# k's fourth block by seven products, with pieces of the second x^T phi(k) batch between them

## The chip, the cores and the metric

One core of a Trainium2 chip. The metric is the device time of the whole kernel in microseconds (us), lower is better. Matrix products run on TensorE (PE), element-wise work on VectorE (DVE) and ScalarE (ACT); SyncE (SP) and GpSimd (POOL) issue the transfers that are spoken of here.

## The reference

Cut to what matters here: x (2048 x 640) goes through a linear attention with 32 heads and through a gated unit, and a sigmoid gate mixes the two.

```
qkv = x @ wqkv;  q, k, v = split(qkv)
phi = lambda t: where(t > 0, t + 1, exp(t)) + 1e-6
kv = einsum("hsd,hse->hde", phi(k), v)
z = einsum("hsd->hd", phi(k))
a = einsum("hqd,hde->hqe", phi(q), kv) / (einsum("hqd,hd->hq", phi(q), z) + 1e-6)
b = (sigmoid(x @ w_gate) * (x @ w_up)) @ w_down
g = sigmoid(x @ gate_w)
out = g * (a @ wo) + (1 - g) * b
```

The part that is changed computes k = x @ wk for some tokens, and x^T phi(k), from which kv follows later.

## The kernel before

Every fp32 product is made of three matmuls of rounded fp32 halves: a tensor is split into a high half (ACT, a copy that rounds) and a low half (DVE, the difference). `mm3` issues the three, `split` the two halves; their lines are the helpers' L202 and L204 (matmul), L214 (ACT) and L218 (DVE, two tensors).

The first phase (to about 134 us) computes k and x^T phi(k). The columns of x^T (640 features, KC = 5 groups of 128) come in chunks of CW = 256 tokens: `xst[:, 0]` has the chunk of one 512-token group, `xst[:, 1]` the matching chunk of the next group. A block is 128 tokens of either side; so a chunk has two blocks, and there are eight blocks (0 to 7) in four chunks. k of a block has two sides (`xst[:, 0]` and `xst[:, 1]`) and two column halves of HW = 322 (320 of k and two columns for the gate), which makes a 2 x 2 block product over the features, plus a fifth feature group:

- `KPlain(b)` computes it plainly: 5 groups x 2 sides x 2 halves x 3 matmuls = 60 matmuls of 322 columns, into four PSUM banks (ch, dd, cc, rot).
- `KBlock(b)` computes it by seven products in Winograd's manner, `s1` to `s7`: 18 terms x 3 = 54 matmuls, into three banks (ch, dd, cc). ch and cc are added to from product to product and copied out between them (`s1`, `s3` and `s5` end with an ACT copy of ch). It needs sums of x's four blocks (tiles xt0 to xt3: `Chunk.sum`, `Chunk.form`) and sums of k's weights (`k_sum`, `k_form` into ksh and ksl), and the difference of the fifth weight rows (`k_fifth_d`, into k5h[2] and k5l[2], read by `s7`).

Before, blocks 0 to 3 are plain and 4 to 7 by seven products, two blocks at a time (a's product, then b's). The plain blocks keep x's groups 0 and 1 of the second side in xt0 (`plain_b12`).

`phi` of a side turns a block's banks into phi(k) (two exp, two relu on ACT, one combining operation on DVE: kr for the first side, kb for the second), `k_split` splits it (pkh, pkl), and `GTBatch.part(u, t0, t1)` adds tokens' products x^T phi(k) into bank u: seven parts (GU), six matmuls of 512 columns (parts 0 to 4) or 320 columns (5 and 6) for each block. The tokens' x (xnst) is split too (xnh, xnl; `queue_xn`). The sum over phi(k) goes by POOL transfers into zacc. A part that is complete is added into gta or gtb by DVE.

There are two PSUM banks of each name (ch, dd, cc, rot), taken in turn: the third tile of a name waits until the readers of the first are done.

The order on each engine is fixed when the program is built. The PE order is the code's order. Splits and sums are queued (`order.add`, `queue_...`) and put between the matmuls by `order.fill()` according to estimated costs, or at once by `order.need(key)`, which issues everything queued up to that key. At run time each engine works through its own list in order and waits for its inputs by semaphores; SP's transfers wait in their list the same way. The next chunk of x is loaded by `chunks[2].load`, behind the loads of xnst in SP's list; each of these is issued when the split that reads its buffer before it is done.

Of the kernel before, what the change touches and what calls it, by code (L numbers as in the profile page):

```python
# [15 lines left out]
P = 128  # L16
S, D, F = 2048, 640, 1536
H, DH = 32, 20
KC = D // P
# [4 lines left out]
HW = HALF + 2  # L24
# [144 lines left out]
def a_cost(w):  # L169
    return 0.19 + w * 0.00084  # L170


def v_cost(w):
    return 0.155 + w * 0.00104
# [3 lines left out]
def gated_mix_kernel(ctx: ExitStack, tc: tile.TileContext, xt, xn, wk, wv, wo, wst_q, wst_f, out_t):  # L178
# [6 lines left out]
    order = Order()  # L185

    def f32(ap):
        return ap.bitcast(F32)
# [23 lines left out]
    def act(out, src, fn, after="", **kw):  # L212
        order.on_act(width(out), after)
        nc.scalar.activation(out, src, fn, **kw)  # L214
# [5 lines left out]
    def vec3(out, a, scalar, b, op0, op1, after=""):  # L220
        order.on_vec(width(out), after)
        nc.vector.scalar_tensor_tensor(out, a, scalar, b, op0=op0, op1=op1)
# [64 lines left out]
    def op_tile(tag, dt=F32R):  # L287
        return p1.tile([P, 2 * HW], dt, name=tag, tag=tag, bufs=6)
# [120 lines left out]
    xc = XForms(px)  # L409
    xc.turned(px)  # L410
    XF = {1: xc}
    b12h, b12l = xc.ft[0]
# [8 lines left out]

    xst_v = [xst[:, b] for b in range(2)]
    chunks = [Chunk(pr, c, xc, xst_v) for pr in range(2) for c in range(TG // CW)]
    for ck in chunks[:2]:
        ck.b12 = (b12h, b12l)
    wk_st = [op_tile(t, F32) for t in ("xnh", "xnh", "xnl", "pkh", "pkl")]
    for k in range(KC):
        nc.sync.dma_start(xst[:, 0, k], xt[0, :, k, :CW])
# [11 lines left out]
    def k_sum(s, j):  # L440
        a11, a21 = wk_st[j][:, lo_h], wk_st[j][:, hi_h]
        a12, a22 = wk_st[2 + j][:, lo_h], wk_st[2 + j][:, hi_h]
        if s == 0:
            add(a22, a21, a22)
        elif s == 2:
            sub(a21, a11, a21)
        elif s == 1:
            sub(a11, a22, a11)
        else:
            sub(a12, a12, a11)  # L450

    def k_form(s, j):
        src = (wk_st[2 + j][:, hi_h], wk_st[j][:, lo_h], wk_st[j][:, hi_h], wk_st[2 + j][:, lo_h])[s]
        split(ksh[:, s, j], ksl[:, s, j], src)
# [19 lines left out]
            return k1h[:, k], k1l[:, k]  # L474
        return (k3h[:, k], k3l[:, k]) if k < 2 else (k2h[:, k - 2], k2l[:, k - 2])

    def queue_ks():
        for s, sums in ((1, (0, 2, 1)), (0, ()), (2, ()), (3, (3,))):
            for j in range(2):
                for t in sums:  # L480
                    order.add(0, v_cost(HW), lambda t=t, j=j: k_sum(t, j))
            for j in range(2):
                order.add(a_cost(HW), v_cost(HW), lambda s=s, j=j: k_form(s, j), ("ks", s))
        order.add(a_cost(HW), 2 * v_cost(HW), k_fifth_d, ("ks", 5))

    XN, PK, KR = {}, {}, {}
    xn_st = {}
# [1 line left out]
    def tok(b, side):  # L489

        pr, j = divmod(b, 4)
        return (2 * pr + side) * 4 + j
# [8 lines left out]
    def split_xn(n):  # L501
        xh, xl = op_tile("xnh"), op_tile("xnl")
        split(xh[:, :D], xl[:, :D], xn_st.pop(n)[0])
        XN[tok(n // 2, n % 2)] = (xh, xl)
        order.then(lambda: load_xn(n + 2))

    def queue_xn(b):
        for n in (2 * b, 2 * b + 1):
            order.add(a_cost(D), v_cost(D), lambda n=n: split_xn(n), ("xn", b), lambda n=n: xn_st[n][1])
# [116 lines left out]
    def k_split(i, after=""):  # L626
        r = KR.pop(i)
        ph, pl = op_tile("pkh"), op_tile("pkl")
        vh, vl = (t[:, :D].rearrange(view2, j=2) for t in (ph, pl))
        act(vh, r, AF.Copy, after, bias=EPS)  # L630
        at = order.act

        def low():
            order.vec = max(order.vec, at)
            vec3(vl, r, EPS, f32(vh), OP.add, OP.subtract)
        order.then(low)
        PK[i] = (ph, pl)
# [10 lines left out]
    def z_step():  # L648

        n = z_tree.pop(0)  # L650
        if n < 0:
            for d in range(4):
                nc.gpsimd.dma_start(z4[d * H:(d + 1) * H], z_dram[:4].rearrange("r (h u d) -> d h u r", u=KC, d=4)[d])
        elif n == 0:
            nc.gpsimd.dma_start(z_dram, zacc[:32])
        else:
            t = zacc if n > 16 else z_dram
            nc.gpsimd.dma_start(t[:n], t[n:2 * n], accum_op=OP.add)

    def queue_split(b):  # L660
        for s in range(2):
            order.add(a_cost(D), v_cost(D), lambda s=s: k_split(tok(b, s)), ("pk", b))
# [46 lines left out]
    def load_w():  # L709
        if w_loads and w_loads[0] in w_hold:  # L710
            w_skipped.append(1)
        elif w_loads:
            n = kind, i = w_loads.pop(0)
            t = pg.tile([P, 2, D], F32, name="wst", tag="wst", bufs=2)
            if kind == "f":
                nc.sync.dma_start(t, wst_f[i, :, 0:2])
            elif kind == "q":
                nc.sync.dma_start(t, wst_q[:, 2 * (i % 2):2 * (i % 2) + 2])
            else:
                nc.sync.dma_start(t[:, 0], wst_q[:, KC - 1])  # L720
            WST[n], W_AT[n] = t, max(order.pe, order.vec) + 4.0
# [62 lines left out]
    def queue_su(n):  # L784
        def fn():
            w_form(n, "V", WST[n][:, 1, :4 * P])
            order.then(load_w)
        order.add(a_cost(4 * P), v_cost(4 * P), fn, ("V", n), lambda: w_free("V"))
# [46 lines left out]
    b1.phi_a()  # L835
    b1.phi_b()
    chunks[1].queue(sums=False)
    queue_xn(1)
    queue_split(1)
    g = GTBatch(0, [0])  # L840
# [6 lines left out]
    batches = {1: [1, 2], 2: [3, 4], 3: [5, 6]}  # L847

    for c in range(1, 4):
        ck = chunks[c]  # L850
        if c == 1:
            a, b = KPlain(2), KPlain(3)
            order.need((ck, "plain"))
            queue_ks()
            queue_xn(2)
            for k in range(KC):
                a.k(k)
                order.fill()
            a.phi_a()
            for k in range(KC):  # L860
                b.k(k)
                order.fill()
                if k == 0:
                    a.phi_b()
            order.need(("ks", 5))
            for t in range(2):
                k_split(tok(2, t))
        else:
            a, b = KBlock(2 * c), KBlock(2 * c + 1)
            for n in range(1, 6):  # L870
                order.need((ck, n))
                if c == 2 and n >= 3:
                    order.need(("ks", (1, 0, 2)[n - 3]))
                getattr(a, f"s{n}")()
                getattr(b, f"s{n}")()
                if n == 2:
                    queue_xn(2 * c)
            order.need((ck, 6))
            if c == 2:
                order.need(("ks", 5))  # L880
            if c + 1 < len(chunks):
                chunks[c + 1].load()
            else:
                nx = [Chunk(0, i, None, xst_v) for i in range(2)]
            a.s6()
            a.s7()
            a.sum_b()
            a.phi_a()
            b.s6()
            a.phi_b()  # L890
            order.need(("pk", 2 * c - 1))
            k_split(tok(2 * c, 0))
            b.s7()
            b.sum_b()
            k_split(tok(2 * c, 1))
        if c == 3:
            pa_cm.__exit__(None, None, None)
            pg_cm = tc.tile_pool(name="pg", bufs=1, side="right", reuse_waits="tile")
            pg = pg_cm.__enter__()
            for _ in range(2):  # L900
                load_w()
        elif c == 1:
            chunks[2].load(lag=6.0)
        g = GTBatch(c, batches[c])
        order.need(("xn", 2 * c))
        if c < 3:
            chunks[c + 1].queue()
        else:
            queue_xn(7)
        held = 3 if c < 3 else 4  # L910
        for u in range(held):
            g.part(u, 0, 2, ("rot", "dd", "ch", "cc")[u])
            if u == 0:
                b.phi_a()
            if u == 1:
                b.phi_b()
        queue_split(2 * c + 1)
        if c < 3:
            queue_xn(2 * c + 1)
        else:  # L920
            queue_w(("u", 1))
            queue_w(("q", 0))
            queue_su(("q", 0))
        for u in range(held):
            g.part(u, 2, 3)
            order.fill()
        for u in range(GU):
            g.part(u, 3 if u < held else 0, 4)
            order.fill()
            if c == 3 and u == 5:  # L930
                z_step()
# [327 lines left out]
    last = QLast(1)  # L1259
# [12 lines left out]
    for n, b in enumerate(blocks):  # L1272
# [20 lines left out]
        else:  # L1293
            last = QLast(0)
# [587 lines left out]
    for turn in SEQ:  # L1882
# [5 lines left out]
        for i, q, pp in jobs:  # L1888
            b = now[i]
            k = hk + pp * len(now) + i  # L1890
# [55 lines left out]
```

## Time and profile before

| | us |
|---|---|
| time, median of 3 runs (lowest to highest) | 728.12 (727.79 to 728.7) |
| the profiled execution's own time | 727.9 |
| its span | 726.2 |
| PE busy | 721.5 |
| DVE busy | 486.4 |
| ACT busy | 320.4 |
| POOL busy | 129.1 |

The time is that of the whole launch; the span runs from the first to the last instruction in the trace, and all starts below are counted from its beginning. Block 2 stands at 31.69 to 40.59 on PE, block 3 at 40.59 to 49.49, the batch of blocks 1 and 2 at 49.49 to 66.88, and blocks 4 and 5 at 66.88 to 82.90. A row in order of time gives the start, the duration, the engine, the line, the operation, out<-in, the shape, and in brackets the idle time before it and what ended it.

### The profile page before, as it was taken

The page shows a single profiled execution, that of the slowest core. Times are in us where ns is not written, and L with a number is a line of the kernel's source. Part 1 is how long each engine was busy: PE and PEld are TensorE (multiplying, and loading weights), DVE is VectorE, ACT ScalarE, POOL GpSimd, SP SyncE. Part 2 cuts the span into 40 slices and gives each one's busy share as a digit, 9 for nine tenths or more (in the row PEclk, how much of TensorE's full clock was granted, in tenths as well). Part 3 has the DMA queues.
Part 4 walks back from the last instruction along what each step waited for, and adds up shares of the span by engine and source line. Part 5 has one row for each costly group of instructions (what it writes and reads, how often), then busy time and mean ns, then how long its engine had stood idle before and what let it go on. Part 6 is the DMA issues. An engine that isn't in the chain of part 4 may idle for free.

```text
span 726.2 us, 9528 instructions
## 1 busy us (share of the span) xinstructions
PE 721.5 (99%) x3411; PEld 608.9 (84%) x3411; DVE 486.4 (67%) x773; ACT 320.4 (44%) x541; POOL 129.1 (18%) x221
## 2 busy tenths in 40 slices
PE   9999999999999999999999999999999999999997
PEld 8999998888888888888888888888888888888886
DVE  4878576868773788678879778796866664434340
ACT  5764628167766233332323242233366644424321
POOL 0311010222430023113224223340200000010000
PEclk9999999999999999999999999999999999999999
DMA  7553537697545464656578658474988966466431
GB/s 253 126 145 76 163 55 212 144 309 228 204 159 196 152 215 137 185 190 226 197 255 314 223 187 288 160 269 130 323 305 264 330 224 194 156 210 198 147 113 72
DMA packets 62563, 144.05 MB, mean 198 GB/s; under 512 B 11150, under 2 KB 24494, under 8 KB 62517
## 3 DMA queue, kind: packets, MB, share of 16 engines
q1 hardware_dynamic: 43829, 88.50, 38.7%
q0 software_dynamic: 18544, 54.83, 23.2%
q8 instruction: 26, 0.43, 0.3%
q14 instruction: 20, 0.16, 0.1%
q10 hardware_dynamic: 144, 0.13, 0.1%
HBM read 89.81 MB, written 49.84 MB: 192 GB/s over the span
## 4 chain that ended last, share of the span: by engine, by line
PE 99%; DVE 0%; ACT 0%; issue 0%
PE ch L204 18%; PE cc L204 17%; PE rot L204 16%; PE dd L204 14%; PE ch L202 9%; PE cc L202 8%; PE rot L202 8%; PE dd L202 7%; PE cc L1131 1%; PE rot L295 1%; PE cc L1212 0%; DVE ot L218 0%; ACT ot L214 0%
## 5 line engine op out<-in xcount | busy, mean ns | idle before, releaser
L218 DVE TENSOR_TENSOR hf<-hw,hf 128x1024 fp32r<-128x1024 f32 x54 | 65.8, 1223 | 68.8 <-ACT hf L214 68.6
L214 ACT ACTIVATE hf<-hw 128x1024 fp32r<-128x1024 f32 x54 | 56.8, 1057 | 54.5 <-PE rot L204 32.1
L218 DVE TENSOR_TENSOR c<-cc,c 128x512 f32<-128x512 f32 x56 | 37.7, 686 | 46.2 <-PE cc L204 40.5
L204 PE MATMUL ch<-hf,wa 128*128 128x512 f32 x160 | 49.3, 389 | 0.0
L204 PE MATMUL dd<-hf,wa 128*128 128x512 f32 x160 | 49.3, 389 | 0.0
L1732 POOL DMA_DIRECT2D out_t<-ot x18 | 9.7, 540 | 183.8 <-DVE ot L218 180.8
L214 ACT ACTIVATE wG<-wst 128x640 fp32r<-128x640 f32 x17 | 12.4, 737 | 65.0 <-PE dd L204 65.0
L214 ACT ACTIVATE c<-ch 128x512 f32<-128x512 f32 x32 | 19.1, 597 | 49.6 <-PE ch L204 44.8
L204 PE MATMUL rot<-hf,wa 128*128 128x512 f32 x128 | 39.4, 389 | 0.0
L204 PE MATMUL cc<-hf,wa 128*128 128x512 f32 x128 | 39.4, 389 | 0.0
L202 PE MATMUL dd<-xrh,wG 128*128 128x512 f32 x90 | 35.4, 394 | 0.0
L204 PEld LDWEIGHTS ch<-hf,wa 128*128 128x128 f32 x160 | 30.0, 188 | 6.3
L204 PEld LDWEIGHTS dd<-hf,wa 128*128 128x128 f32 x160 | 30.0, 188 | 6.3
L204 PE MATMUL dd<-xrh,wG 128*128 128x512 f32 x90 | 35.0, 389 | 0.0
L204 PE MATMUL dd<-xrl,wG 128*128 128x512 f32 x90 | 35.0, 389 | 0.0
L218 DVE TENSOR_TENSOR c<-c,om 128x512 f32<-128x512 f32 x48 | 33.1, 692 | 1.6
L202 PE MATMUL cc<-xbh,wS 128*128 128x512 f32 x84 | 32.7, 389 | 0.0
L204 PE MATMUL cc<-xbl,wS 128*128 128x512 f32 x84 | 32.7, 389 | 0.0
L204 PE MATMUL cc<-xbh,wS 128*128 128x512 f32 x84 | 32.7, 389 | 0.0
L202 PE MATMUL dd<-hf,wa 128*128 128x512 f32 x80 | 31.1, 389 | 0.0
L202 PE MATMUL ch<-hf,wa 128*128 128x512 f32 x80 | 31.1, 389 | 0.0
L214 ACT ACTIVATE c<-rot 128x512 f32<-128x512 f32 x24 | 14.2, 597 | 38.3 <-PE rot L204 31.0
(471 smaller groups left out, 2088.5 us busy)
## 6 DMA issues: line engine op xcount, KB each, us to landing
hf<-p_dram SPq DMA_DIRECT2D x16, 512.0 KB, 5.3
hw<-h1T SPq DMA_DIRECT2D x16, 512.0 KB, 5.0
hw<-h0T SPq DMA_DIRECT2D x16, 512.0 KB, 4.5
wst<-wst_f SPq DMA_DIRECT2D x12, 640.0 KB, 4.5
xst<-xt SPq DMA_DIRECT2D x10, 640.0 KB, 7.5
h1T<-c POOLq DMA_DIRECT2D x24, 256.0 KB, 2.7
h0T<-c POOLq DMA_DIRECT2D x24, 256.0 KB, 3.1
hw<-h1B SPq DMA_DIRECT2D x11, 512.0 KB, 4.6
```

Of the source, the lines that this page charges most:

```text
L202: nc.tensor.matmul(o, l_hi, r, start=first, stop=False, skip_group_check=True)
L204: nc.tensor.matmul(out, a, b, start=False, stop=last and n == 1, skip_group_check=True)
L214: nc.scalar.activation(out, src, fn, **kw)
L218: nc.vector.tensor_tensor(out, a, b, op=op)
L295: nc.tensor.matmul(wps[:, :w], ones_w[:, :P], ones_w[:, :w], start=True, stop=True)
L1131: nc.tensor.matmul(ps[:w, b0:b1], v[:, m, :w], g(m), start=(m == 0), stop=(m == KC - 1))
L1732: (eng or nc.gpsimd).dma_start(out_t[o * P:(o + 1) * P, g * TG + c0:g * TG + c1], t[:, c0:c1])
```

## The change

Block 3 becomes a `KBlock` while block 2 stays plain. The second half of chunk 1 (128 tokens of either side) gets a chunk object of its own, `half[1]`, whose sums and splits are queued behind the plain splits; `half[0]` has block 2's plain split of x's groups 0 and 1. The sums and splits of k's weights, queued after block 1 as before, are queued in two pieces around `half[1]`'s. Parts 0, 1 and 2 of the batch of blocks 1 and 2 are started for block 1 between the products of block 3: part 0 and part 1 after `s2`, part 2 after `s4`. phi and the split of block 2 stand between the products as well, phi of block 3's first side after `s6`, that of its second side after `s7`.

```diff
-    for ck in chunks[:2]:
-        ck.b12 = (b12h, b12l)
+    chunks[0].b12 = (b12h, b12l)
+    half = [Chunk(0, 2 + i, xc, [x[:, :, i * P:(i + 1) * P] for x in xst_v], P, (b12h, b12l)) for i in range(2)]
...
-    def queue_ks():
-        for s, sums in ((1, (0, 2, 1)), (0, ()), (2, ()), (3, (3,))):
+    def queue_ks(end):
+        for s, sums in ((3, (3,)),) if end else ((1, (0, 2, 1)), (0, ()), (2, ())):
...
-        order.add(a_cost(HW), 2 * v_cost(HW), k_fifth_d, ("ks", 5))
+        if end:
+            order.add(a_cost(HW), 2 * v_cost(HW), k_fifth_d, ("ks", 5))
...
     chunks[1].queue(sums=False)
+    order.add(a_cost(2 * P), v_cost(2 * P), half[0].plain_b12, (half[0], "plain"))
...
         if c == 1:
-            a, b = KPlain(2), KPlain(3)
-            order.need((ck, "plain"))
-            queue_ks()
+            a, b = KPlain(2), KBlock(3)
+            order.need((half[0], "plain"))
+            half[1].queue_sums(last=False)
+            queue_ks(False)
+            half[1].queue_sums(first=False)
+            queue_ks(True)
             queue_xn(2)
+            g = GTBatch(c, batches[c])
             for k in range(KC):
                 a.k(k)
                 order.fill()
+            b.s1()
             a.phi_a()
-            for k in range(KC):
-                b.k(k)
-                order.fill()
-                if k == 0:
-                    a.phi_b()
+            b.s2()
+            a.phi_b()
+            order.fill()
+            order.need(("xn", 1))
+            order.need(("pk", 1))
+            g.part(0, 0, 2, "rot")
+            order.fill()
+            g.part(1, 0, 2, "dd")
+            order.need((half[1], 3))
+            order.need(("ks", 1))
+            b.s3()
+            k_split(tok(2, 0))
+            order.need((half[1], 4))
+            order.need(("ks", 0))
+            b.s4()
+            g.part(2, 0, 2, "ch")
+            k_split(tok(2, 1))
+            order.need((half[1], 5))
+            order.need(("ks", 2))
+            b.s5()
+            order.need((half[1], 6))
+            b.s6()
+            b.phi_a()
             order.need(("ks", 5))
-            for t in range(2):
-                k_split(tok(2, t))
+            b.s7()
+            b.sum_b()
+            b.phi_b()
...
-        for u in range(held):
+        for u in range(held if c > 1 else 0):
             g.part(u, 0, 2, ("rot", "dd", "ch", "cc")[u])
```

Three places in the engines' lists. First PE, where block 3 and the batch meet. Before, block 3 ends and the batch begins (dd, cc, rot with numbers are single PSUM tiles; pkh and pkl are phi(k)'s halves, xnh and xnl those of x):

```order
L204 MATMUL cc_482<-k5h_154,xbl_135 128x322
L202 MATMUL rot_483<-k5h_154,xbh_134 128x322
L204 MATMUL rot_483<-k5l_155,xbh_134 128x322
L204 MATMUL rot_483<-k5h_154,xbl_135 128x322
L202 MATMUL rot_692<-pkh_506,xnh_497 128x512
L204 MATMUL rot_692<-pkl_507,xnh_497 128x512
```

Now, part 1 of the batch (dd_631, the third dd tile in turn; block 2 had dd_477, block 3 has dd_481) stands ahead of product 3:

```order
L204 MATMUL rot_624<-pkh_511,xnl_500 128x512
L202 MATMUL dd_631<-pkh_505,xnh_496 128x512
L204 MATMUL dd_631<-pkl_506,xnh_496 128x512
L204 MATMUL dd_631<-pkh_505,xnl_497 128x512
L202 MATMUL dd_631<-pkh_511,xnh_499 128x512
L204 MATMUL dd_631<-pkl_512,xnh_499 128x512
L204 MATMUL dd_631<-pkh_511,xnl_500 128x512
L202 MATMUL ch_480<-ksh_152,xt1h_142 128x322
L204 MATMUL ch_480<-ksl_153,xt1h_142 128x322
```

The batch's first three parts moved from behind block 3 to between its products.

Second DVE, the last sums and splits of k and the fifth row's difference (pkl<-pkl and k5l; the raw rows of wk lie in tiles named xnh, xnl, pkh and pkl). Before, beside plain block 3:

```order
L218 TENSOR_TENSOR pkh<-pkh,xnh 128x322
L218 TENSOR_TENSOR ksl<-xnl,ksh 128x322
L218 TENSOR_TENSOR pkl<-pkl 128x322
L218 TENSOR_TENSOR ksl<-pkh,ksh 128x322
L218 TENSOR_TENSOR k5l<-pkl,k5h 128x322
```

Now:

```order
L218 TENSOR_TENSOR ksl<-xnh,ksh 128x322 x2
L218 TENSOR_TENSOR xst<-xst 128x2x128
L218 TENSOR_TENSOR xt3l<-xst,xt3h 128x2x128
L218 TENSOR_TENSOR xnl<-xnl,xnh 128x322
L218 TENSOR_TENSOR pkh<-pkh,xnh 128x322
L218 TENSOR_TENSOR kb<-cc,kb 128x322
L218 TENSOR_TENSOR ksl<-xnl,ksh 128x322
L218 TENSOR_TENSOR ksl<-pkh,ksh 128x322
L526 COPY logit<-ta 128x1
L222 SCALAR_TENSOR_TENSOR kr<-ke,kr 128x640
L218 TENSOR_TENSOR pkl<-pkl 128x322
L218 TENSOR_TENSOR k5l<-pkl,k5h 128x322
```

The difference moved behind phi of block 3's first side (logit<-ta, kr<-ke).

Third DVE again, the batch's results (gta<-rot, dd, ch, rot) and the splits of the third chunk (xal, xrl, xbl). Before:

```order
L218 TENSOR_TENSOR xal<-xst,xah 128x2x256
L218 TENSOR_TENSOR gta<-rot,gta 128x512
L218 TENSOR_TENSOR gta<-dd,gta 128x512
L218 TENSOR_TENSOR gta<-ch,gta 128x512
L218 TENSOR_TENSOR xrl<-xst,xrh 128x3x256
L218 TENSOR_TENSOR xbl<-xst,xbh 128x3x256
L218 TENSOR_TENSOR xst<-xst 128x512
L218 TENSOR_TENSOR gta<-rot,gta 128x512
```

Now:

```order
L218 TENSOR_TENSOR gta<-rot,gta 128x512
L218 TENSOR_TENSOR gta<-dd,gta 128x512
L218 TENSOR_TENSOR gta<-ch,gta 128x512
L218 TENSOR_TENSOR gta<-rot,gta 128x512
L218 TENSOR_TENSOR xal<-xst,xah 128x2x256
L218 TENSOR_TENSOR xrl<-xst,xrh 128x3x256
L218 TENSOR_TENSOR xbl<-xst,xbh 128x3x256
L218 TENSOR_TENSOR xst<-xst 128x512
L218 TENSOR_TENSOR gta<-rot,gta 128x512
```

The third chunk's splits moved behind the sums of parts 0 to 3, and the fifth part's sum (the last row) still stands behind them. In SP's list the third chunk's two loads of xst stood behind five loads of xnst since the chunk before, and now stand behind six.

3 lines of the change are left out of this document (2 added, 1 removed).

## The prediction

> **What bounds the kernel now.** I read the page's busy times and its chain that ended last, then the stretches around the change, then the rows in order of time on TensorE (PE), VectorE (DVE), ScalarE (ACT) and the DMA queue of SyncE (SP).
>
> ```profile
> PE 721.5 (99%) x3411; PEld 608.9 (84%) x3411; DVE 486.4 (67%) x773; ACT 320.4 (44%) x541; POOL 129.1 (18%) x221
> PE 99%; DVE 0%; ACT 0%; issue 0%
> ```
>
> ```profile
> 31.69:40.59 8.90, 8.90 (x63) 8.90 (x61) 7.33 (x14) 5.03 (x11) 1.20 (x1) 1.00 0.51 118
> 40.59:49.49 8.90, 8.90 (x62) 8.90 (x61) 8.14 (x17) 7.63 (x20) 2.10 (x2) 1.00 0.28 52
> 49.49:66.88 17.39, 17.39 (x86) 14.78 (x85) 12.38 (x21) 5.64 (x12) 2.09 (x2) 1.00 0.65 163
> ```
>
> The three stretches (columns: length, then PE, PEld, DVE, ACT, POOL busy, granted clock, DMA share, GB/s) are block 2, block 3 and the second x^T phi(k) batch. PE is busy for all of each, and the chain is PE alone, so whatever PE gains or waits here reaches the end undiluted. DVE (8.14 of 8.90) and ACT (7.63 of 8.90) are nearly full beside block 3. A matmul's duration overlaps the next one's, so the pace is read from starts:
>
> ```profile
> 40.59 0.31 PE L202 MATMUL ch<-k1h,xah 128*128 128x322 f32 x1
> 40.74 0.31 PE L204 MATMUL ch<-k1h,xal 128*128 128x322 f32 x1
> ...
> 49.35 0.31 PE L204 MATMUL rot<-k5h,xbl 128*128 128x322 f32 x1
> 49.49 0.39 PE L202 MATMUL rot<-pkh,xnh 128*128 128x512 f32 x1
> 49.72 0.40 PE L204 MATMUL rot<-pkl,xnh 128*128 128x512 f32 x1
> ```
>
> Block 3 is 60 matmuls in 8.90 us, 0.148 each, with no gap; a 512-wide one takes 0.232.
>
> **The change, part by part.** *Removed:* seven products take 54 matmuls instead of 60. 6 x 0.148 = 0.89 us, all on PE's path. The second half of the plain x12 split goes too; it lay on DVE and ACT where nobody waited, worth nothing.
>
> *Moved and added.* The batch's first three parts keep their 18 matmuls. Block 3 now needs, ahead of its products, three sums and four splits of x for 128 columns, and the sums and splits of k, which before were first read in block 4. All of it goes through DVE and ACT in written order, so I walk the new order with the durations of these rows:
>
> ```profile
> 35.93 0.48 DVE L218 TENSOR_TENSOR xnl<-xnh,xnl 128x322 f32<-128x322 f32 x1
> 36.45 0.49 DVE L218 TENSOR_TENSOR xnh<-xnh 128x322 f32<-128x322 f32 x1
> ...
> 42.23 0.83 DVE L222 SCALAR_TENSOR_TENSOR kr<-ke,kr 128x640 f32<-128x640 f32 x1 [0.16 <-ACT kr L214]
> ...
> 45.09 0.49 DVE L218 TENSOR_TENSOR pkl<-pkl 128x322 f32<-128x322 f32 x1
> ...
> 46.12 0.50 DVE L218 TENSOR_TENSOR k5l<-pkl,k5h 128x322 fp32r<-128x322 f32 x1
> 46.75 0.83 DVE L218 TENSOR_TENSOR xnl<-xnst,xnh 128x640 fp32r<-128x640 f32 x1
> 47.49 0.82 DVE L222 SCALAR_TENSOR_TENSOR pkl<-kr,pkh 128x640 fp32r<-128x640 f32 x1
> 48.23 0.82 DVE L222 SCALAR_TENSOR_TENSOR pkl<-kb,pkh 128x640 fp32r<-128x640 f32 x1
> ```
>
> ```profile
> 9.08 0.42 DVE L218 TENSOR_TENSOR xt0l<-xst,xt0h 128x256 fp32r<-128x256 f32 x1
> 9.41 0.42 DVE L218 TENSOR_TENSOR xrl<-xst,xrh 128x256 fp32r<-128x256 f32 x1
> ```
>
> ```profile
> 10.04 0.40 ACT L214 ACTIVATE xbh<-xst 128x256 fp32r<-128x256 f32 x1
> ...
> 39.35 0.46 ACT L214 ACTIVATE ksh<-xnl 128x322 fp32r<-128x322 f32 x1
> 39.72 0.46 ACT L214 ACTIVATE ksh<-pkh 128x322 fp32r<-128x322 f32 x1
> ...
> 41.76 0.44 ACT L214 ACTIVATE kr<-dd 128x320 f32<-128x320 f32 x1
> ...
> 45.61 0.47 ACT L214 ACTIVATE k5h<-pkl 128x322 fp32r<-128x322 f32 x1 [0.34 <-DVE pkl L218]
> ...
> 46.62 0.72 ACT L214 ACTIVATE pkh<-kr 128x640 fp32r<-128x640 f32 x1
> 47.25 0.72 ACT L214 ACTIVATE pkh<-kb 128x640 fp32r<-128x640 f32 x1
> ...
> 72.44 0.44 ACT L214 ACTIVATE kb<-ch 128x322 f32<-128x322 f32 x1 [1.19 <-PE ch L204]
> ```
>
> ```profile
> 72.09 0.31 PE L204 MATMUL ch<-ksh,xt1l 128*128 128x322 f32 x1
> ```
>
> Independent work on an engine starts 0.09 before the end of what runs (39.35 to 39.72), dependent work and another engine about 0.03 after it (36.45; kr<-dd ends 42.20, kr starts 42.23). What a matmul wrote can be read about 0.35 after its start (72.09 to 72.44).
>
> Wait 1, part 1 of the batch. It takes block 2's dd bank, which the ACT copy kr<-dd of phi frees. The x work enters DVE's queue ahead of the sums of k: three sums of 256 elements (each waits for the last: 3 x 0.45), the ACT split behind them (0.4), three low halves (3 x 0.33): 2.8 us, so the first sum of k moves from 35.93 to 38.75. ACT's splits of k wait for these sums and phi stands behind them, so kr<-dd ends at 42.20 + 2.8 = 45.0. PE is there at 40.59 + 15 x 0.148 + 6 x 0.232 = 44.2. Wait: 0.9.
>
> Wait 2, product 5. Its two low halves of k stand on DVE behind the split of block 2's phi, and that on ACT behind the copy of product 3. Product 3 ends at 45.05 + 1.39 + 0.89 = 47.3; copy 47.65, the two pkh 48.0 and 48.65, pkl 48.75 and 49.5, low halves 50.25 and 50.65. PE needs the first after 50.2 and gets it at 50.75: 0.55.
>
> Wait 3, product 6. It writes the bank of product 5, which ACT must first copy: last matmul's start 51.35, then 0.35, the copy 0.46 (held a moment by the x split ahead of it), 0.03: 52.3 against 51.5: 0.8. Pairs of blocks hide this copy under the other block's product; a single block doesn't.
>
> Waits 4 to 6, product 7. Its low halves of k come 0.25 late. Then its third term needs the fifth row's difference, which both engines have behind phi of block 3, and that starts when product 6 ends (53.6): ACT kr<-ch ends 54.95, DVE kr starts and hands over 0.74 later, pkl 55.7 to 56.2, ACT k5h to 56.7, DVE k5l to 57.25. PE stands there from 54.8: 1.95, and 0.4 more for the low half.
>
> Wait 7, parts 0 to 2 with block 2's rows: DVE's xnl comes behind k5l, done 58.2: 0.2. Waits 1 to 7: 5.0 us. I leave out the added latency of a PE that has to start again, at most 0.1 each by my estimate from these spacings; it goes into the range.
>
> Wait 8, far from the edit. SP's queue has both xn loads of the next pair ahead of the third chunk's x load, and each waits for one of the two xnl above. The load of x, whose first half was issued at 48.0 before, is issued at about 59.6 and 60.2 (xnl done 58.2 and 59.0). DVE has the sum of the batch's part 3, then xal, xrl, xbl, a sum of xst, and only then the add of part 4, which frees the rot bank for part 6, the batch's last.
>
> ```profile
> L340 SPq DMA_DIRECT2D xst<-xt x4: 551/590/837, 48.0 to 79.8; - x4
> ...
> DMA to landing us min/median/max: 6.9/7.7/9.4
> ```
>
> ```profile
> 56.34 0.85 ACT L214 ACTIVATE xbh<-xst 128x768 fp32r<-128x768 f32 x1 [0.50 <-DMA xst<-xt]
> ```
>
> ```profile
> 59.49 0.95 DVE L218 TENSOR_TENSOR xbl<-xst,xbh 128x768 fp32r<-128x768 f32 x1
> 60.36 0.69 DVE L218 TENSOR_TENSOR xst<-xst 128x512 f32<-128x512 f32 x1
> 60.96 0.69 DVE L218 TENSOR_TENSOR gta<-rot,gta 128x512 f32<-128x512 f32 x1
> ```
>
> From landing to the freed bank: 0.87 + 0.87 + 0.60 + 0.72 = 3.06 us. PE wants it at 69.26 (66.88 less the last part's 12 x 0.148 = 65.1, less 0.89, plus 5.0). So the wait is zero if the second half lands within 6.0 us of its issue, 0.9 at 6.9, 1.7 at 7.7, 3.4 at 9.4. I take 8.1, an estimate: nearest to the middle of the row, and a little above it because two xn loads instead of one stand just ahead. Wait 8: 2.1, bounds 0.9 and 3.4.
>
> The Trainium skill, "DMA: Bandwidth & Descriptors", section on the anatomy of one DMA, puts a transfer at about 2.0 us plus its bytes at 436 GB/s. By that rule, as an estimate, both halves (1.31 MB) would land 5 us after the first issue, wait 8 would be zero and the total 732.2. The trace doesn't agree (6.9 to 9.4 us for one half), and I go by the trace; the first rival covers the other outcome.
>
> Behind it the third chunk's splits are on time: xt1 is ready about 74 and first read at about 77.5 (73.1 + 30 x 0.148). Later order is the same in both kernels. POOL's queue keeps its adds into zacc in their order:
>
> ```profile
> zacc<-kb POOLq DMA_DIRECT2D x2, 320.0 KB, 5.8
> ```
>
> The four of blocks 2 and 3, one after the other at 5.8 from about 46 on, end by 69.2; their buffers are wanted again in product 3 of block 4, after 77.5. I cost them at nothing; one later than that would cost its lateness.
>
> Sum: -0.89 + 5.0 + 2.1 = +6.2 us. The profiled execution took 727.9 (span 726.2), which gives 734.1; the median of the runs, 728.12, lies 0.2 above it: 734.3. About 0.2% (1.5 us) is what a measurement here can tell from no change.
>
> **The rivals.**
>
> Early transfer. Wait 8 vanishes because x lands within 6.0 us. For: the batch leaves the DMA engines share to spare (0.65 in its stretch). Against: four of four such loads took longer. Time: 728.1 - 0.9 + 5.0 = 732.2, from 731 to 733.
>
> Cover holds. The seven products find every input ready, and only the 0.89 shows: 727.2, not slower. The place is product 7 with its difference: it turns if ACT and DVE finish that chain before PE has done product 6. For: PE never waited here before, and DVE was idle 1.57 us beside block 2. Against: the chain starts from product 6's own result, and the order, not the load, puts it there. It decides only if all waits together stay under 0.9 + 1.5 = 2.4 us.
>
> Slow clock. A long wait makes PE run slower afterwards. The start shows such a phase, 0.26 a matmul instead of 0.148, until 6.03, 5.2 us from PE's first matmul:
>
> ```profile
> 0.85 3.79 PE rot L295 x9
> ```
>
> ```profile
> 4.72 0.47 PE L204 MATMUL ch<-k1h,xal 128*128 128x322 f32 x1
> 4.99 0.46 PE L204 MATMUL ch<-k1l,xah 128*128 128x322 f32 x1
> ...
> 6.03 0.31 PE L202 MATMUL ch<-k1h,xah 128*128 128x322 f32 x1
> ```
>
> One such phase costs 5.2 x (1 - 0.148/0.26) = 2.2 us: 736.5. Against: the longest waits, 2.4 (split by one matmul) and 2.1, are less than half as long as that phase, and the granted clock is 1.00 in each stretch quoted; so this rival is small. The Trainium skill, "TensorE: Matmul & The Clock Gate", Part 1, says that the clock halves after an idle window of about 3.4 us; by that rule only wait 8 at its upper bound comes near.
>
> **How the numbers follow.** Forecast case, all eight waits: 0.64, own range 732.2 (products' waits 4.1, wait 8 at 0.9) to 736.4 (5.8 and 3.4). Early transfer 0.20. Cover holds 0.06. Slow clock or a still later load 0.07. Something less than half of the waits, at 729 to 731: 0.03. The range, 731.2 to 737.0, leaves out the last case and cover below and the upper half of the slow clock above. Slower by over 0.2%: 0.93; within 0.2%: 0.06; faster, for which there is no more than 0.89 to gain: 0.01.
>
> **What would show it.** 54 matmuls of 322 columns in block 3. PE waits, by the rows: for ACT kr<-dd ahead of part 1, for DVE ksl in product 5, for ACT in product 6, and the longest of the products for k5h in product 7. One wait of about 2 us for DVE ahead of part 6 of the batch, with ACT xbh released by the x load just before. Block 4 starting at about 73.1 instead of 66.88, and the rest shifted by that. I am wrong if PE shows no wait in product 7, or if x is issued well before 59.

## The result, and the profile after

The changed kernel takes 735.89 us (median of 6 runs, 734.4 to 737.41) against 727.95 (727.62 to 729.08): ratio 1.0107, 95% interval 1.0097 to 1.0117, so 1.1% slower. The forecast was 734.3, range 731.2 to 737.0. The profiled execution, the fastest of the six, took 734.4 us, span 732.3. (In experiment 8 below one run of eleven, the profiled one, took 899.96 us at a granted clock of 0.753; it has no part in the ratio given there.) Busy times and the chain that ended last, of the changed kernel:

```profile
PE 724.2 (99%) x3405; PEld 609.9 (83%) x3405; DVE 490.4 (67%) x784; ACT 322.8 (44%) x546; POOL 129.1 (18%) x221
PE 92%; ACT 1%; DVE 1%; issue 0%
```

Six matmuls fewer, and yet PE is busy 2.7 us longer: matmuls that run slower count as busy, and so does the end of a matmul ahead of a wait (its row lasts 0.31 us where the next one would start after 0.148). The chain is no longer PE alone. The stretches by engine, for block 2 and for block 3 with the batch behind it (columns as before: length, PE, PEld, DVE, ACT, POOL, granted clock, DMA share, GB/s):

```profile
31.84:40.74 8.90, 8.90 (x62) 8.90 (x61) 6.99 (x14) 4.22 (x9) 1.20 (x1) 1.00 0.50 115
40.74:73.01 32.27, 28.78 (x141) 24.03 (x139) 22.97 (x44) 15.55 (x35) 4.19 (x4) 0.95 0.44 102
```

Block 2 is unchanged. Block 3 and the batch take 32.27 us instead of 26.29 (40.59 to 66.88 before): the whole loss of 6.0 lies here. PE stands still for parts of it, and its granted clock (the share of its full clock that PE was given, on average) is 0.95. What PE waited for, from the list of waits (total, times, longest):

```profile
PE cc L202 <- ACT k5h L214: 1.9, 1, 1.9
...
PE dd L202 <- ACT kr L214: 0.7, 1, 0.7
PE ch L202 <- ACT kb L214: 0.5, 1, 0.5
PE ch L204 <- DVE ksl L218: 0.3, 1, 0.3
```

These are the forecast's waits in product 7, ahead of part 1, ahead of product 6 and in product 5. In order of time on PE:

```profile
45.20 0.50 PE L202 MATMUL dd<-pkh,xnh 128*128 128x512 f32 x1 [0.66 <-ACT kr L214]
...
50.96 0.41 PE L204 MATMUL ch<-ksl,xt2h 128*128 128x322 f32 x1 [0.33 <-DVE ksl L218]
...
52.50 0.42 PE L202 MATMUL ch<-k2h,xt3h 128*128 128x322 f32 x1 [0.53 <-ACT kb L214]
...
57.08 0.41 PE L202 MATMUL cc<-k5h,xbh 128*128 128x322 f32 x1 [1.85 <-ACT k5h L214]
57.61 0.63 PE L204 MATMUL cc<-k5l,xbh 128*128 128x322 f32 x1
...
58.31 0.63 PE L202 MATMUL rot<-pkh,xnh 128*128 128x512 f32 x1
...
60.45 0.63 PE L204 MATMUL dd<-pkh,xnl 128*128 128x512 f32 x1
60.87 0.44 PE L202 MATMUL ch<-pkh,xnh 128*128 128x512 f32 x1
...
70.84 0.30 PE L204 MATMUL rot<-xnh,pkl 128*128 128x320 f32 x1
71.13 0.42 PE L202 MATMUL rot<-xnh,pkh 128*128 128x320 f32 x1
```

From 57.6 to 60.9 the 512-wide matmuls start every 0.427 us (58.31 to 60.87 in six), not every 0.232. The granted clock in stretches of 3.4 us (the third column from the right) says it directly:

```profile
50.70:54.10 3.40, 2.61 (x15) 2.27 (x15) 2.92 (x9) 1.87 (x5) 1.00 (x1) 1.00 0.60 96
54.10:57.50 3.40, 1.54 (x8) 0.93 (x6) 2.20 (x6) 2.10 (x6) 0.90 (x1) 1.00 0.00 0
57.50:60.90 3.40, 3.29 (x9) 2.73 (x10) 2.17 (x5) 1.97 (x4) 0.00 (x0) 0.51 0.90 192
60.90:64.30 3.40, 3.40 (x16) 2.79 (x15) 2.61 (x4) 0.29 (x1) 1.19 (x1) 0.99 0.90 299
```

PE is granted half its clock for one stretch of 3.4 us (half pace below), behind a stretch in which it was busy for only 1.54. And ahead of part 6 (71.13) the long wait that was forecast is a gap of 0.14, though the x load came as late as forecast (the issue, ACT's split of the second half, the add that frees the bank):

```profile
59.66 1.23 SPq L340 DMA_DIRECT2D xst<-xt  x2
...
68.03 0.85 ACT L214 ACTIVATE xbh<-xst 128x768 fp32r<-128x768 f32 x1 [0.84 <-DMA xst<-xt]
70.39 0.68 DVE L218 TENSOR_TENSOR gta<-rot,gta 128x512 f32<-128x512 f32 x1
```

### The profile page after: what moved, and what is told of

Its sections match the earlier page's. It is cut to its first block, busy times and chain, and to the rows that moved or that the text cites. A ratio compares the mean times of both kernels' runs of the same rounds, so it can differ in the third digit from the quotient of the medians.

```text
span 732.3 us, 9532 instructions
## 1 busy us (share of the span) xinstructions
PE 724.2 (99%) x3405; PEld 609.9 (83%) x3405; DVE 490.4 (67%) x784; ACT 322.8 (44%) x546; POOL 129.1 (18%) x221
## 4 chain that ended last, share of the span: by engine, by line
PE 92%; ACT 1%; DVE 1%; issue 0%
PE ch L204 17%; PE cc L204 16%; PE rot L204 15%; PE dd L204 12%; PE ch L202 9%; PE cc L202 8%; PE rot L202 8%; PE dd L202 6%; PE cc L1158 1%; ACT ke L214 0%; DVE pkl L222 0%; ACT kr L214 0%; ACT ksh L214 0%; ACT kb L214 0%; DVE kr L222 0%
## 5 line engine op out<-in xcount | busy, mean ns | idle before, releaser
L218 DVE TENSOR_TENSOR hf<-hf 128x256 f32<-128x256 f32 (+2 forms) x53 | 30.0, 568 | 1.2
```

The costliest lines, as they stand in the source:

```text
L218: nc.vector.tensor_tensor(out, a, b, op=op)
```

## The experiments

Each edit is against the changed kernel unless said otherwise. All times are medians; the kernel before measured 727.9 to 728.0 beside all of them.

### 1. The changed kernel again

No edit.

> The changed kernel once more, nothing edited, with a profile of its own. Theory: its times spread over 3 us (734.4 to 737.4) because the x load of the third chunk is issued at 59.7 and the add that frees the bank for part 6 hangs on its landing: times again between 734 and 737.5, and in this profile a landing that differs from 7.7 us moves the wait ahead of part 6 by the same amount. Rival: the spread comes from the slow phase of TensorE behind product 7, which is there in some runs alone: then this profile shows no phase of 0.26 to 0.29 us a matmul, and a time about 1.5 us lower.

Measured 735.05 us (734.6 to 736.99), ratio 1.0103 (1.0089 to 1.0116); profiled execution 735.0, span 732.9. The half pace is there again, and not in some runs alone: all ten runs of this kernel, here and above, have a mean clock of 0.997 or 0.998 (one such stretch in 733 us takes 0.0023 off). The second half of x landed 8.6 us after its issue instead of 7.7, and the rows move by that:

```profile
68.65 0.85 ACT L214 ACTIVATE xbh<-xst 128x768 fp32r<-128x768 f32 x1 [0.40 <-DMA xst<-xt]
...
71.01 0.68 DVE L218 TENSOR_TENSOR gta<-rot,gta 128x512 f32<-128x512 f32 x1
...
71.75 0.42 PE L202 MATMUL rot<-xnh,pkh 128*128 128x320 f32 x1 [1.04 <-DVE gta L218]
```

The gap ahead of part 6 is 1.2 us here and was 0.14, for a landing 0.9 later. The theory holds: the landing of x sets the end of this stretch and with it the spread.

### 2. The x load ahead of the xn loads

```
         order.need((half[1], 6))
+        chunks[2].load()
         b.s6()
...
-        chunks[2].load(lag=6.0)
+        chunks[2].at = max(order.pe, order.vec) + 6.0
```

> The change, with the third chunk's x load put in SP's list ahead of the two xn loads (right behind the last use of the second chunk's x), everything else in the same order. Theory (products' waits plus a slow phase of PE behind the 2 us wait in product 7, with the late x load only hidden behind them): x is issued at about 53 and landed by 61, part 6 finds its bank free, but the waits of product 5, 6 and 7 and the slow phase stay, so block 4 starts at 72.7 to 73.0 where the change has 73.3, and the time falls by no more than 0.3 us against the same profile (734.4), to 733.7 to 734.2. Rival (the late x load sets when block 4 can start, and the waits ahead of it are free): block 4 starts at 69 or earlier and the time falls by 3 us or more, to 731 or less.

Measured 733.97 us (733.77 to 734.15), ratio 1.0082 (1.0067 to 1.0097); span 731.7. The load is issued at 51.92, both halves land 4.1 us after their issue instead of 6.1 and 7.7, and nothing waits ahead of part 6. The wait in product 7 and the half pace behind it stay:

```profile
54.80:58.20 3.40, 1.67 (x6) 1.07 (x7) 2.73 (x5) 1.73 (x3) 0.90 (x1) 1.00 1.03 309
58.20:61.60 3.40, 3.40 (x9) 2.61 (x8) 1.77 (x4) 2.55 (x4) 0.00 (x0) 0.51 0.91 242
```

The times now spread over 0.4 us instead of 3. The late load costs 1.1 us against experiment 1's median (1.9 against that of the first six runs), not the 2.1 of the forecast, since it lies beside the half pace. In the profiled runs it costs nothing: from block 3 to block 4 PE takes 32.31 us here (40.09 to 72.40) and 32.27 in the changed kernel's trace. What is gained is gained over the runs in which x lands later than there.

### 3. The fifth row's difference early, x still late

```
         b.s3()
+        was = order.act, order.vec
+        k_fifth_d()
+        order.act, order.vec = was
         k_split(tok(2, 0))
```

(In its old place an entry with the same costs and no instructions, so that the rest of the order stays.)

> The change, with the difference of k's fifth row and its split moved up behind product 3; the x load stays late. Theory: the wait of 1.9 and 0.4 in product 7 goes, and with it the slow phase (no wait above 1 us is left among the products); parts 0 to 2 then wait 0.9 for xn instead of 0.2, product 5 0.9 instead of 0.5. PE reaches part 6 at about 68 and there waits for the late x load, 1.7 us (x issued at 58.4 and 59.0). Total waits 5.5: 727.9 - 0.9 + 5.5 = 732.5, bounds 731.5 and 734. Rival (slow phase has nothing to do with the wait): the 0.43 us spacing of 512-column matmuls still appears near 58, and the time is 733.5 or more.

Measured 735.8 us (733.89 to 737.03), ratio 1.0106 (1.0085 to 1.0127): a miss. Taking the longest wait away gained nothing. PE has no long wait in product 7 and no half pace at 58, but it comes to part 6 earlier, and x is as late as before (the longest wait, and the stretches around it):

```profile
PE rot L202 <- DVE gta L218: 2.6, 1, 2.6
```

```profile
65.30:68.70 3.40, 2.69 (x17) 2.26 (x15) 1.93 (x3) 1.77 (x3) 0.00 (x0) 1.00 0.71 137
68.70:72.10 3.40, 1.46 (x10) 1.46 (x11) 3.40 (x6) 0.00 (x0) 0.00 (x0) 1.00 0.00 0
72.10:75.50 3.40, 3.40 (x15) 3.40 (x15) 1.77 (x4) 2.01 (x4) 0.00 (x0) 0.50 0.00 0
```

The wait moved ahead of part 6, and the half pace followed it there. I had left the half pace out of that expectation. One of the four runs, the fastest (733.89), has a mean clock of 1.000 and so no half pace; the others have 0.997 or 0.998 and took 735.37 to 737.03.

### 4. Experiment 2 with PE kept busy in product 7

```
         if self.b == 3:
             prod(self.cc[:, :HW], t[:2], False)
             junk = ps_tile("cc")
             for _ in range(8):
                 nc.tensor.matmul(junk, ones_w[:, :P], ones_w, start=True, stop=True)
             t = t[2:]
```

> a2 with eight 512-column bf16 matmuls into a bank of its own between the second and the third term of product 7, so that PE works while it would wait; their results are not used. Theory: the same waits for k5h end at the same moment, but PE keeps its full pace behind them: 0.232 per 512-column matmul at 58 to 61 where the change shows 0.43. Against a2 it gains what the slow phase costs, 1.4 to 1.7 us: 727.9 - 0.9 + 5.0 = 732.0, bounds 731.3 and 732.8. Rival (the slow pace comes from what the matmuls read or from other traffic at that moment): the pace stays at 0.43 and the time is that of a2.

Measured 732.61 us (732.49 to 732.86), ratio 1.0064 (1.0049 to 1.0079). Eight matmuls of constants fill the wait for k5h; k5h comes no earlier, yet 1.36 us are gained, since the half pace is gone:

```profile
58.20:61.60 3.40, 3.40 (x15) 2.73 (x15) 1.98 (x5) 2.15 (x4) 0.00 (x0) 1.00 0.98 260
```

### 5. Experiments 2 and 3 together

> a2 and a3 together: early fifth row and early x load. Theory: neither the long wait nor the slow phase nor the wait at part 6; what is left is 0.9 ahead of part 1, 0.9 in product 5, 0.8 ahead of product 6, 0.25 in product 7 and 0.9 at the parts for xn: 3.8 us. 727.9 - 0.9 + 3.8 = 730.8, bounds 730.2 and 731.6. Rival (the interleaving costs by itself, for instance by contention, and not by these waits): the time stays above 732.

Measured 731.05 us (730.96 to 731.3), ratio 1.0043 (1.0028 to 1.0058). Neither edit alone gives more than 1.9 us, both give 4.0 to 4.8: either wait comes with a half pace and hides behind the other. What is left are the waits ahead of part 1, in product 5, ahead of product 6, and 0.42 and 0.40 behind product 7 (for ACT xnh and DVE xnl).

### 6. Experiment 2 with part 1 behind product 4

```
-            g.part(1, 0, 2, "dd")
             order.need((half[1], 3))
...
             b.s4()
+            g.part(1, 0, 2, "dd")
             g.part(2, 0, 2, "ch")
```

> The changed kernel with the x load early (as in the second experiment) and part 1 behind product 4 instead of ahead of product 3. By the walk the 0.9 wait for block 2's dd bank goes, the wait in product 5 falls from 0.55 to 0.1, that ahead of product 6 stays 0.8, and the waits in product 7 stay 0.25, 1.95 and 0.4. Against 733.97 with the x load early alone that is 1.35 less. Theory (the slow phase is set off by the 2 us wait in product 7 alone): it stays, 732.4 to 732.8. Rival (it needs the waits of the 10 us before as well): no slow phase, 731.0 to 731.5.

Measured 732.67 us (732.58 to 733.01), ratio 1.0066 (1.0052 to 1.0079): 1.30 less than experiment 2, of 1.35 expected. The waits ahead of part 1 and in product 5 are gone, and the half pace behind product 7 stays, so it doesn't need those two.

### 7. The parts behind the products

```
-            g.part(0, 0, 2, "rot")
-            g.part(1, 0, 2, "dd")
...
-            g.part(2, 0, 2, "ch")
...
-        for u in range(held if c > 1 else 0):
+        for u in range(held):
```

> The changed kernel with block 3's seven products kept, and the second batch's parts 0 to 2 behind all of them instead of between them. By the walk TensorE then waits 0.96 ahead of product 3 and 0.8 and 2.5 in and ahead of product 5 (the splits of k by ScalarE and VectorE), 0.8 ahead of product 6, 0.25, 1.95 and 0.4 in product 7, in all 7.6 instead of 5.0, and none ahead of part 6, since the batch ends 2.6 later while the x load is issued at about the same 58.3 and 58.9. Theory (the parts between the products cover 2.6 us of the waits, and TensorE falls to half pace behind the 2.5 and the 1.95): 727.9 - 0.9 + 7.6 + 0.6 for the restarts + 1.5 for each phase: 736.7 with one, 738.2 with two. Rival (the parts between the products only shift the waits, since VectorE and ScalarE have the same work to do by the end of product 7): 735 to 736, as the changed kernel.

Measured 737.42 us (736.47 to 738.24), ratio 1.0129 (1.0114 to 1.0144), between the theory's two values. The profiled run (738.14) has two stretches of half pace, and all four runs have the same mean clock, 0.995; what makes the spread between them isn't shown.

```profile
PE ch L204 <- DVE ksl L218: 2.2, 1, 2.2
PE cc L202 <- ACT k5h L214: 1.8, 1, 1.8
```

```profile
47.30:50.70 3.40, 1.01 (x5) 0.75 (x5) 2.79 (x7) 1.67 (x5) 0.16 (x1) 1.00 0.52 96
50.70:54.10 3.40, 3.05 (x11) 3.06 (x12) 2.48 (x7) 1.76 (x5) 1.05 (x1) 0.53 0.60 96
54.10:57.50 3.40, 1.45 (x7) 0.97 (x7) 1.81 (x4) 2.10 (x6) 0.90 (x1) 0.97 0.01 0
57.50:60.90 3.40, 3.40 (x10) 2.75 (x11) 2.03 (x4) 1.97 (x3) 0.00 (x0) 0.53 0.98 225
```

So this part of the change helps: with the parts between the products the kernel is 1.5 to 2.4 us faster (735.89 and 735.05 against 737.42). This includes one stretch of half pace less.

### 8 and 9. The seven products with every wait covered

```
             b.s4()
+            g.part(1, 0, 2, "dd")
             order.need((half[1], 5))
             order.need(("ks", 2))
             b.s5()
+            g.part(2, 0, 2, "ch")
             order.need((half[1], 6))
             b.s6()
+            chunks[2].load()
             order.need(("ks", 5))
+            order.items.pop(0)
+            split_xn(4)
+            k_split(tok(2, 0))
             b.phi_a()
+            g.part(3, 0, 2, "rot")
             b.s7()
             b.sum_b()
+            k_split(tok(2, 1))
+            order.need(("xn", 2))
             b.phi_b()
...
+            g.part(u, 3 if u < held else 0, 4, "dd" if (c, u) == (1, 4) else "rot")
```

(The old places of part 1, part 2, the splits of block 2's phi and the x load go, and `held`, the number of parts begun early, is 4 here instead of 3.)

> Seven products for k's fourth block as in the changed kernel, but every wait that the walk named is given cover: part 1 stands behind product 4 and part 2 behind product 5 (its copy is hidden), part 3 is begun too, between product 6 and product 7; the low halves of k for product 5 stand ahead of the splits of block 2's phi, the fifth row's difference and split ahead of phi of block 3, one xn split and one split of phi ahead of it too; the third chunk's x load is issued behind product 6, ahead of the xn loads; part 4 goes to the dd bank. Theory (the 6 us are waits that the order of the work makes, the seven products themselves save 6 x 0.148 = 0.89): by the same walk no wait is left, 727.0 to 727.6 against 727.9 before, ratio 0.9988 to 0.9996, TensorE without a gap from 40.6 to 66. Rival (the added sums and splits on VectorE and ScalarE cost time in any order, since both engines are nearly full there): about 2 us of waits stay, 728.5 to 730.

Measured 726.99 us, ratio 0.9988 (0.9979 to 0.9997). The profile was taken from a second run of the same kernel:

> The covered kernel once more, unchanged, for a profile of it at the full granted clock. Theory: 727.0 again, span about 725.1, and between 40.6 and 66 no start of a matmul later than its pace by more than 0.1 us, block 4 starting at 66.0 (66.88 less 0.89). Rival: the ratio of 0.9988 came from the runs of before, and gaps of some tenths are left: time 727.5 to 728.

Measured 726.97 us (726.56 to 727.46), ratio 0.9986 (0.9976 to 0.9996), span 725.0. Block 3 with its four parts, and the rest of the batch:

```profile
40.33:53.93 13.60, 13.60 (x80) 12.54 (x79) 11.21 (x26) 10.07 (x27) 2.10 (x2) 1.00 0.38 95
53.93:65.79 11.86, 11.86 (x62) 10.28 (x61) 10.86 (x18) 5.63 (x10) 2.09 (x2) 1.00 0.62 149
```

PE is busy for all of both at clock 1.00; 40.33 to 65.79 is 25.46 us against 26.29 before, 0.83 less of the 0.89 that six matmuls are worth. No start between is more than 0.06 us behind its pace; block 4 starts at 65.79 (66.0 expected). DVE (11.21 of 13.60) and ACT (10.07) have all the added sums and splits to do and do them in time. This version beats the kernel before by about 0.9 us (by the interval 0.3 to 1.7) and the changed kernel by 8 to 9.

### 10. Made waits of four lengths

In the covered kernel, at parts 4 and 6 of the third and the fourth batch:

```
+    def probe(n):
+        ps = ps_tile("cc")
+        t = p1.tile([P, 512], mybir.dt.bfloat16, name="idle", tag="ta", bufs=2)
+        nc.tensor.matmul(ps, ones_w[:, :P], ones_w, start=True, stop=True)
+        for _ in range(n):
+            nc.scalar.activation(t, ps, AF.Copy)
+        nc.tensor.matmul(ps, t[:, :P], ones_w, start=True, stop=True)
```

> The covered kernel with four made waits in the third and fourth x^T phi(k) batch, where TensorE has no gap and ScalarE little to do: a 512-column matmul of constants, 2, 3, 4 or 5 copies of its result by ScalarE one after the other, and a second matmul that reads the copy. By 0.35 us to the first copy, 0.54 for each further one and 0.66 for the last, less 0.23, the waits are 1.3, 1.9, 2.4 and 2.9 us (order in time: 2 copies at the third batch's part 4, 3 at its part 6, 4 and 5 in the fourth batch); with the added matmuls that is 10.4 us. Theory (a wait of about 2.3 us makes TensorE run at half pace for some 3.5 us behind it, which costs 1.4 to 1.6 us): the matmuls behind the 4 and 5 copies go at 0.29 instead of 0.148 or 0.43 instead of 0.232, those behind 2 and 3 copies don't; time 740.5 to 741.5 if the covered kernel takes 727.3. Rival A (TensorE's pace doesn't hang on the length of the wait): no phase, 738. Rival B (it needs a wait above 2.9 us or an earlier history): no phase either, 738; a phase behind 3 copies too would put the bound under 1.9 us: 742 to 743.

Measured 741.08 us (739.91 to 742.46); the runs' mean clocks lie between 0.993 and 1.000, so they had different numbers of half-pace stretches; the run at 1.000 (740.2) had none, although the same four waits were made in it. In the profiled one (742.46) the waits are 1.32, 1.95, 2.58 and 3.21, and the pace is halved behind all but the first. The expected time was met, but the reason wasn't: a wait of 1.95 was to be free. The last of the four shows when the half pace begins:

```profile
146.62 0.39 PE L860 MATMUL cc<-const-bfloat16-1.0,idle 128*128 128x512 bf16 x1 [3.21 <-ACT idle L859]
146.66 0.50 PE L202 MATMUL rot<-xnh,pkh 128*128 128x320 f32 x1
147.00 0.32 PE L204 MATMUL rot<-xnl,pkh 128*128 128x320 f32 x1
...
147.93 0.47 PE L204 MATMUL rot<-xnl,pkh 128*128 128x320 f32 x1
148.19 0.47 PE L204 MATMUL rot<-xnh,pkl 128*128 128x320 f32 x1
```

```profile
144.40:147.80 3.40, 1.18 (x8) 1.16 (x9) 0.00 (x0) 3.30 (x7) 1.06 (x2) 1.00 0.23 24
147.80:151.20 3.40, 3.40 (x12) 3.01 (x11) 1.72 (x3) 0.43 (x1) 0.00 (x0) 0.50 0.84 239
```

PE restarts at 146.62 and goes at full pace for 1.2 us; only then, at 147.8, its clock is halved, for 3.4 us. So it isn't the wait's end that sets it off. The rows fit the end of a stretch of fixed length in which PE was busy too little.

### 11. The same made wait four times

`PROBE` gives 3 copies at all four places.

> The covered kernel with the same made wait four times: a matmul of constants, 3 copies of its result by ScalarE, a matmul that reads the copy, at the third and the fourth x^T phi(k) batch's parts 4 and 6. Each wait measured 1.95 us before. Theory (the clock is decided anew every 3.4 us on a fixed raster, by how much of the last 3.4 us TensorE was busy, and half pace holds for the whole next 3.4 us): a wait of 1.95 slows TensorE where most of it lies in one such window, and not where it straddles two, so in one profile some of the four places have a phase of half pace and others none, phases begin and end on a raster of 3.4 us, and the runs spread by about 1.6 us a phase: 735.5 (none) to 742 (all four), the profile's mean clock 1.000 to 0.990. Rival (a length of wait decides, with a threshold between 1.5 and 1.95 us): all four places have the phase in every run, 741 to 742 with a spread under 0.5 us.

Measured 740.56 us (739.99 to 741.32), each run at a mean clock of 0.995. My 735.5 for no phase was too low: 727.0 and four waits of 1.95 make 734.8, which leaves 0.7 for the eight added matmuls (0.46 at each place) and the restarts. The four waits come out at 2.18, 1.95, 2.18 and 1.95 us. Half pace follows the second and the third and not the first and the fourth. The stretches around the first two waits, and then around the other two, are cut where the trace's record of the clock changes and at steps of 3.41 us from there:

```profile
94.59:98.00 3.41, 1.53 (x7) 1.02 (x6) 2.48 (x5) 1.55 (x3) 1.20 (x1) 1.00 0.16 24
98.00:101.41 3.41, 3.11 (x21) 3.09 (x22) 1.61 (x3) 2.02 (x4) 0.00 (x0) 1.00 0.47 72
101.42:104.83 3.41, 1.46 (x10) 1.04 (x9) 1.52 (x3) 2.29 (x4) 0.00 (x0) 1.00 0.01 2
104.83:108.24 3.41, 3.41 (x15) 3.41 (x14) 1.65 (x2) 1.48 (x4) 0.00 (x0) 0.50 0.33 96
...
135.55:138.96 3.41, 1.23 (x7) 0.83 (x8) 1.53 (x3) 2.41 (x5) 0.24 (x1) 1.00 0.52 96
138.96:142.37 3.41, 3.41 (x15) 3.41 (x14) 1.42 (x3) 1.26 (x3) 0.97 (x1) 0.50 0.62 96
142.37:145.79 3.42, 1.71 (x11) 1.30 (x10) 1.12 (x2) 1.61 (x3) 0.86 (x1) 1.00 0.31 48
145.79:149.20 3.41, 3.17 (x19) 2.94 (x20) 1.48 (x3) 1.85 (x4) 0.79 (x1) 1.00 0.28 74
```

A length of wait can't tell these apart: of either length, one wait is followed by half pace and one isn't. A raster can. The two halved stretches begin 34.13 us apart (104.83 and 138.96), ten times 3.413; in experiment 7 the two begin 6.82 apart (50.89 and 57.71), in experiment 10 the three 34.13 and 10.24 (103.46, 137.59 and 147.83): two, ten and three times 3.413.

The share that decides is known only roughly. With edges set in this way in all traces, half pace followed every stretch with less than 1.5 us of PE busy and none with 1.82 or more; between these it went both ways (half pace behind 1.51 in the changed kernel and 1.74 in experiment 2, full pace behind 1.53 and 1.71 here). The busy time of PE is modelled in part, and where exactly the stretch is cut isn't shown.

## Why the prediction was right, and where its sum was not

The sign and the place were right, and the time lies in the range, 1.6 us above the forecast by the median (735.89 against 734.3). By gaps between PE's starts beyond its pace, in the profiled run of the changed kernel, the fastest of its six:

| step | forecast | measured |
|---|---|---|
| six matmuls fewer | -0.89 | -0.89 |
| wait 1, ahead of part 1 | 0.9 | 0.83 |
| wait 2, in product 5 | 0.55 | 0.49 |
| wait 3, ahead of product 6 | 0.8 | 0.68 |
| waits 4 to 6, in product 7 | 0.25 + 1.95 + 0.4 | 0.13 + 2.00 + 0.38 |
| wait 7, xnl | 0.2 | none, covered by the half pace |
| slow restarts | left out, in the range | 0.42 (four of about 0.1) |
| half pace behind product 7 | a rival at 0.07 | 1.58 |
| wait 8, ahead of part 6 | 2.1 | 0.25 with its restart |
| sum | +6.2 | +5.87; 5.98 with gaps too small to list |

*The walk* through DVE's and ACT's order gave the waits 1 to 6 to within 0.12 each, from durations of the kernel before alone. The runs confirm them as causes: with the fifth row early the 2 us wait in product 7 goes (experiment 3), with part 1 behind product 4 the waits 1 and 2 do (6), and with the whole order mended no wait is left and the six matmuls show (8 and 9). That the seven products were slower here lay in the order, not in the added sums and splits.

*Wait 8* was the mis-sized step: 2.1 forecast, 0.25 there. Its own parts were right. The load was issued at 59.7 (59.6 forecast), the second half landed after 7.7 us (8.1), and the chain from there to part 6 took 3.10 (3.06). What was wrong was PE's arrival: 69.26 forecast, 70.99 measured, because the half pace had cost it 1.58 on the way. The two lie side by side, and the later one sets the end: without the half pace PE would have come at 69.4 and waited 1.7 us for the same 71.1. That is why the total came out though this term failed, and why experiments 2 and 3 gain so little one by one. In part it was luck: a cost that the sum had put at nothing, the half pace, happened to fit into the 1.7 us that PE would have waited anyway. The sign of a wait of about 2 us ahead of part 6 failed. The rule of the Trainium skill, "DMA: Bandwidth & Descriptors", anatomy of one DMA, that the prediction set aside for the trace is stated there for transfers issued by GpSimd; this load is issued by SyncE, and its second half took 7.7 us.

*The slow-clock rival* was set too low: it came true in every run of the changed kernel, and only wait 8 hid it from the sum. Its reason was wrong too: I compared the length of the waits with that of the slow phase at the start. By experiments 10 and 11 it is how little PE was busy in a stretch of 3.41 us on a fixed raster (under 1.5 us always enough, 1.82 or more never, in these traces); experiment 4, which keeps PE busy through the same wait, takes the half pace away. The wait of 1.85 in product 7, with the gap of 0.38 behind it, was enough here, and the price was 1.58, not 2.2. The Trainium skill, "TensorE: Matmul & The Clock Gate", Part 1, speaks of a free-running window of 4096 cycles, about 3.4 us: these runs agree with its length (3.413 us) and with its not being tied to the kernel's events (the first full clock comes at 3.65 us of the span in experiment 2 and at 6.51 in experiment 7). Its condition, an idle window, does not fit: a window a little over half idle was enough (1.51 us busy in the changed kernel).

*Early transfer*, the first rival, was worked out to 732.2 without wait 8. Experiment 2 made just that and took 733.97: the half pace that it had hidden remained. *Cover holds* was rightly small for the order as it was. *POOL's transfers*, costed at nothing, cost nothing: from 71.4 on no PE gap is longer than 0.1 up to 145 us.

What stays open: the median of the first six runs (735.89) lies 1.5 above the profiled one. Experiment 1 shows one such step (a landing of x 0.9 later, a gap 1.06 longer), and the load's early issue takes the spread away. Why the landing differs from run to run isn't shown, nor where exactly between 1.5 and 1.8 us of PE busy the half pace sets in.

## What to carry to other kernels

Fewer matmuls pay only if the sums and splits that they need stand ahead of everything that PE reads later: walk the order of each engine with measured durations, and give each product whose result another engine must copy something else to cover it. Where two late things meet at one point, take both away before judging either. Keep PE well over half busy in every 3.4 us, if need be with matmuls of constants, since a wait of 2 us here cost 1.6 us more behind it.

## What the runs showed of the hardware that I had not expected

- Half the clock for 3.41 us behind a stretch of 3.41 us with about half of PE's time busy or less (1.0 to 1.7 us), on a raster of its own: in experiment 11 a wait of 2.18 us and one of 1.95 us were each free once, and each cost about 1.5 us once (12 or 13 matmuls at 0.267 instead of 0.148).
- A matmul that PE starts behind a wait is followed by the next 0.10 or 0.11 us later than the pace, wherever that next one neither waits itself nor runs at half pace (0.19 behind the made waits of experiments 10 and 11).
- The same x load of two halves lands in 4.1 to 4.3 us (median of the two) where it is issued ahead of the xn loads in experiments 2, 4, 5 and 9, and in 6.1 to 8.6 right behind them (issued at 57.8 to 60.3). Being ahead isn't enough: in experiment 6 it is ahead of them too and takes 6.1, issued at 50.86, 0.6 us behind a transfer into zacc. Whether that transfer is the reason isn't tested.
